# Attention and routed experts on one core: the last value rows read by a casting DMA, the routing steps moved within the first head pair, the gathered rows transposed one score group later

## The chip, the cores and the metric

The kernel runs on one core of one Trainium2 chip. The metric is the device time of one execution in microseconds (us). Each engine of the core works through its own list of instructions in order: TensorE (PE: matmuls and, beside them, weight loads), VectorE (DVE), ScalarE (ACT), GpSimd (POOL) and SyncE (SP, which here only issues DMAs). They wait for each other through semaphores. DMAs are issued from SP, ACT and POOL; those of POOL run on the queue that the profile calls software_dynamic, those of SP and ACT on hardware_dynamic queues.

## The reference

```python
scores = scale * np.matmul(q, k.transpose(0, 1, 3, 2))       # q, k, v: 8 x 8 x 576 x 64, float32
scores = scores + bias.transpose(2, 0, 1)[None, :, :, :]     # bias from |i - j| through a table of 32 buckets
attn = np.exp(scores - max) / (sum + 1e-09)
x = np.matmul(attn, v)                                       # laid out as 4608 tokens x 512
expert_idx = token_ids * np.int64(2654435761) % np.int64(E)  # E = 8 experts
for e in range(E):                                           # rows of expert e
    out[mask] = np.maximum(xe @ w1[e], 0.0) @ w2[e]          # w1: 512 x 1024, w2: 1024 x 512
```

Eight batches of eight heads go through attention; each of the 4608 resulting token rows then goes through the two matrices of one expert, which the token's id alone decides.

## The kernel before, in words

**Attention.** The work goes by head pairs: n = 0 to 31 is batch n // 4, pair m = n % 4 of its heads. For each pair, `scores` (line 484) makes score blocks in four groups g = 0 to 3, each in one of two PSUM buffers `ps`; ACT takes the exp of each group into `att` (lines 513 and 507). `band` (line 518) multiplies the blocks near the diagonal by the exp of the bias, from `ebd` (line 532), on DVE. `av_steps(n)` (line 560) multiplies `att` with the values in two halves (token tiles 0 to 2, then 3 and 4), divides by the row sums and writes `x_all` (lines 579, 589, 590); it is a generator, and the main loop (line 812) advances it by counted matmuls between the score groups of the next pair. So the order of all five engines is written out by hand (`tc.manual_schedule`), and each engine keeps it.

**Loads.** q, k and v come in as fp32, four pairs ahead, on SP (`load`, `load_v`); DVE casts q and k to fp16 (`cast_q`, `cast_k`, lines 274 and 283), PE transposes them (lines 457 and 472), DVE copies the results to `qt` and `kz` (lines 465, 478, 479). ACT casts the first 512 value rows of each head to `vt` (line 289). The last 64 value rows of all heads of a batch come in by `load_vs` (line 257) to an fp32 buffer `vsf` and are cast by POOL in `cast_vs` (line 264) to `vs`, which has one buffer for even and one for odd batches. For batch b + 1 the load stands in the loop at pair m = 1 of batch b and the cast at m = 3; the first matmul that reads it is that of `av_steps(4b + 4)`, advanced during pair 4b + 5.

**Routing.** `route` (line 296) is a generator too: it takes the expert of each token from the ids (`te`, line 299), casts and transposes them (`tef`, `tps`, `ef`), makes one-hot columns (`oh`, line 327), counts them with two matmuls (line 338), a scan (line 342) and a subtraction (line 348), and ends in `ds2`, the slot of each token. Before the main loop it is advanced to the subtraction; the rest comes one step a pair from n = 5. From pair 13 on POOL scatters the tokens' names into `t_id` by 40 indirect DMAs (`name_slot`, line 618), each behind a `pace` copy (line 603) that waits for a reciprocal `rcp` of the pair. At n = 28 SP loads the finished list as `xid` (line 836).

**The hand-over.** SP stores the attention rows of a batch to `t_x` (`store`, line 631), for batch 6 at pair 29. At n = 30 POOL gathers the first expert's 640 rows in five chunks of 128 (`gather`, line 151), from batches 0 to 6. In pair 31 `first_rows` (line 421) transposes chunks 1 to 4 on PE (`xr`) and copies them to `xt0` on DVE. After the loop, `first_slots` (line 432) adds the rows of the last batch straight from `x_all` by one-hot matmuls (`xin`). `aux` tiles (`pq`, `pk`, `px`, `tps`, `xr`, `xin`) share two PSUM buffers in turn.

**Experts.** For each expert, eight groups of matmuls `hps` (line 964), relu on ACT, five groups `ops` (line 988), copies on DVE and scattered stores on POOL (line 996).

Of the kernel before, what the change touches and what calls it, by code (L numbers as in the profile page):

```python
# [11 lines left out]
F32 = mybir.dt.float32  # L12
F16 = mybir.dt.float16
I32 = mybir.dt.int32
# [17 lines left out]
def kernel(  # L32
# [160 lines left out]
    with tc.tile_pool(name="at", bufs=1) as at, tc.tile_pool(  # L193
# [16 lines left out]
        kf = [at.tile([PB, 2, 2 * NBLK, D], F32, name=f"kf{i}")  # L210
              for i in range(4)]
        vf = [at.tile([P, 2, NDUO, D], F32, name=f"vf{i}") for i in range(4)]
        vsf = [at.tile([P, NPAIR, D], F32, name=f"vsf{i}") for i in range(2)]
        vt = [at.tile([P, 2 * (NDUO * VN + VO)], F16, name=f"vt{i}")
              for i in range(4)]
        vs = [at.tile([P, NPAIR, VW], F16, name=f"vs{i}") for i in range(2)]
# [37 lines left out]
                    ),  # L254
                )

        def load_vs(b, eng=nc.sync):
            for hh in range(2):
                eng.dma_start(
                    out=vsf[b % 2][D * hh : D * hh + D, :, :],  # L260
                    in_=v[b, hh::2, NB4:].transpose([1, 0, 2]),
                )

        def cast_vs(b):
            for hh in range(2):
                c0 = hh * HP
                nc.gpsimd.tensor_copy(  # L267
                    out=vs[b % 2][D * hh : D * hh + D, :, c0 : c0 + D],
                    in_=vsf[b % 2][D * hh : D * hh + D, :, :],
                )  # L270

        def cast_q(n):
# [21 lines left out]
            )  # L294

        def route():
            rev = raw[:, :, 0].rearrange("b (u o) -> b o u", o=2)[:, :, ::-1]
            for h0, w, u0 in ((0, UA, 0), (QW, UB, UA)):
                nc.vector.tensor_scalar(
                    out=te[:, h0 : h0 + 2 * w].rearrange(  # L300
                        "b (o u) -> b o u", o=2
                    ),
                    in0=rev[:, :, u0 : u0 + w],
                    scalar1=E - 1, scalar2=None, op0=ALU.bitwise_and,
                )
            yield
            nc.gpsimd.memset(tef[:, :].bitcast(I32), 0)
            nc.vector.tensor_copy(out=tef[:B, :], in_=te[:, :])
            yield
            tps = aux([P, NIT, P], F16, "tps")  # L310
            for t in range(NIT):
                nc.tensor.transpose(
                    out=tps[:, t, :], in_=tef[:, i_first[t] : i_first[t] + P],
                    identity=ident[:, :P],
                )
            nc.vector.tensor_tensor(
                out=ef[:, :].rearrange("p (b t) -> p t b", b=B),
                in0=tps[:, :, :B],
                in1=msk[:, :NGT].rearrange("p (b t) -> p t b", b=B),
                op=ALU.add,  # L320
            )
            keep = at.tile([P, E, NGT], F32, name="keep")
            nc.gpsimd.memset(keep[:, :, :], 1.0)
            nc.gpsimd.memset(keep[:, :, 0:1], 0.0)
            yield
            oh = at.tile([P, E, NGT], F16, name="oh")
            nc.vector.tensor_tensor(
                out=oh[:, :, :],
                in0=ef[:, :].unsqueeze(1).to_broadcast([P, E, NGT]),
                in1=msk[:, NGT : NGT + E].unsqueeze(2).to_broadcast([P, E, NGT]),  # L330
                op=ALU.is_equal,
            )
            yield
            EN = E * NGT
            ohf = oh[:, :, :].rearrange("p e g -> p (e g)")
            rps = atp.tile([P, 3, 512], F32, name="rps", tag="ps", bufs=2,
                           space=bass.MemoryType.PSUM)
            nc.tensor.matmul(out=rps[:, 0, :EN], lhsT=cnt[:, P:], rhs=ohf)
            nc.tensor.matmul(out=rps[:, 1, :EN], lhsT=cnt[:, :P], rhs=ohf)
            inc = at.tile([P, E, NGT], F32, name="inc")  # L340
            incf = inc[:, :, :].rearrange("p e g -> p (e g)")
            nc.vector.tensor_tensor_scan(
                out=incf, data0=keep[:, :, :].rearrange("p e g -> p (e g)"),
                data1=rps[:, 0, :EN], initial=0.0, op0=ALU.mult, op1=ALU.add,
            )
            rnk = at.tile([P, E, NGT], F32, name="rnk")
            rnkf = rnk[:, :, :].rearrange("p e g -> p (e g)")
            nc.vector.tensor_tensor(
                out=rnkf, in0=incf, in1=rps[:, 1, :EN], op=ALU.subtract
            )  # L350
            yield
            mx = at.tile([P, 1], F32, name="mx")
            nc.vector.tensor_reduce(
                out=mx[:, :], in_=inc[:, :, NGT - 1],
                axis=mybir.AxisListType.X, op=ALU.max,
            )
            yield
            mxl = at.tile([P, 1], F32, name="mxl")
            nc.vector.tensor_reduce(
                out=mxl[:, :], in_=inc[:, :, NIT - 1],  # L360
                axis=mybir.AxisListType.X, op=ALU.max,
            )
# [27 lines left out]
            yield  # L390
            nc.vector.scalar_tensor_tensor(
                out=ds2[:, :], in0=ovf[:, :], scalar=float(BIG),
                in1=sel[:, :], op0=ALU.mult, op1=ALU.add,
            )
            yield
# [272 lines left out]
        load(0, "qk")  # L668
        load(1, "q")

        def z_init(i, eng=nc.vector):
            eng.memset(kz[i][D:P, :S].bitcast(I32), 0)
            eng.memset(kz[i][:D, S:].bitcast(I32), 0)

        idle = at.tile([P, 512], F16, name="idle")
        nc.vector.memset(idle[:, :].bitcast(I32), 0)
# [36 lines left out]
                )  # L713

        z_init(1)
        FH = FW // 2
        for i in range(2):
            nc.tensor.matmul(
# [41 lines left out]
                )  # L760

        routing = route()
        advance(routing, 1)
        cast_q(0)
        advance(routing, 1)
        cast_k(0)
        load_bias(nc.scalar, 0, 1, 0)
        load_bias(nc.sync, 0, 1, 1)
        transpose_q(0)
        advance(routing, 2)  # L770
        v_init(0)
        vs_init(0)
        transpose_k(0)
        advance(routing, 1)
        load_vs(0, nc.gpsimd)
        z_init(2, nc.gpsimd)
        for i in range(1, 4):
            v_init(i)
        nobody = at.tile([P, NSLOT // P, 2], I32, name="nobody")
        nc.gpsimd.memset(nobody[:, :, :], BIG)  # L780
        load_v(0)
        cast_q(1)
        cast_k(1)
        nc.gpsimd.tensor_copy(out=pace[:, :], in_=kh[1][:1, 0, 0, 0:1])
        for b2 in range(2):
            load_bias(nc.gpsimd, 1, 2, b2)
        cast_vs(0)
        for b2 in range(2):
            load_bias(nc.gpsimd, 2, NPAIR, b2)
        load(1, "v")  # L790
# [21 lines left out]
        for n in range(NP + 1):  # L812
            av = iter(())
            if n > 0:
                av = av_steps(n - 1, finish if n == NP else None)
            if n == NP:
                first_slots(0, NPT - 1)
                advance(av, 99)
                first_slots(NPT - 1, NPT)
# [5 lines left out]
                vs_init(1)  # L825
            if n == 2:
                make_ebs()
            if b + 1 < B and m == 1:
                load_vs(b + 1)
            if b + 1 < B and m == 3:  # L830
                cast_vs(b + 1)
            if n >= 8 and pairs[n][1] == 0:
                store(pairs[n - 8][0], 0, NIT)
            if n == 28:
# [8 lines left out]
            for g in range(NSG + 1):  # L843
# [5 lines left out]
                if n == NP - 2 and g == 0:  # L849
                    gather(0, B - 1)  # L850
                if n == NP - 1:
                    for sc in ((), (1,), (2, 3), (4,))[g]:
                        first_rows(sc)
                if n == 16 and g == 0 or NP - 2 <= n and g in (0, 1, 3):
                    next(hotting, None)
                if n == 0:
                    if g == 1:
                        transpose_q(1)
                        transpose_k(1)
                        band(n, 0)  # L860
                    elif g == 2:
                        band(n, 1)
                        band(n, 2)
                    elif g == 3:
                        cast_v(0)
                        band(n, 3)
# [23 lines left out]
                elif g == 0:  # L890
                    if 2 < n < NP - 1:
                        transpose_k(n + 1)
                    low_bands(n - 1)
                    advance(av, 12)
                elif g == 1:
                    if n == 2:
                        cast_v(2)
                        load_v(6)
                        advance(av, 15)
                        transpose_k(3)  # L900
                        cast_q(4)
                    if n + 2 < NP:
# [1 line left out]
                    if 2 < n < NP - 1:  # L904
                        cast_v(n + 1)
                    if n > 2:
                        advance(av, 15)
                    band(n, 0)
                elif g == 2:
                    if n == 2:  # L910
# [232 lines left out]
```

## Time and profile before

| what | value |
|---|---|
| timed runs | 370.37, 370.32, 369.44 us; median 370.32 |
| the profiled execution | 370.93 us; its span 369.1 us |
| granted TensorE clock | 0.988 |
| PE busy | 323.6 us, 88% |
| DVE busy | 219.1 us, 59% |
| ACT busy | 236.8 us, 64% |
| POOL busy | 188.3 us, 51% |
| DMA | 66.01 MB, mean 179 GB/s |

The busy shares are means over stages with different limits: a head until the first exp (12.13 us), the attention (to 209.27 us, when the last exp ends), and the experts (from 214.08 us). The profile numbers lines as in the kernel printed above. A row of the timeline gives the start, the duration, the engine, the line, the operation, output and inputs, and in brackets the idle time that the engine had before it with what ended it. A wait for several semaphores is put down to the one that came last. "PEld" is the weight load, "issue" is time in which an engine waited for nothing that the profile shows.

### The profile page before, as it was taken

Reading aid. Unit: us, or ns where it says so; the run is one execution under the profiler, and the core shown is the slowest. Engines: PE = TensorE matmul, PEld = TensorE weight load, DVE = VectorE, ACT = ScalarE, POOL = GpSimd, SP = SyncE. Lnnn points to the kernel's source line nnn. Section 1 sums busy time; section 2 is a strip of 40 time slices with the busy share of each in tenths; the row PEclk is TensorE's granted clock in tenths of the full one; section 3 lists DMA queues with packets and bytes.
Section 4 is the critical chain, followed back from the end, with each engine's and each line's share of the span. In section 5 each row is a group of like instructions: output and inputs, shape, how many; then the busy total and the mean of one; then the engine's idle time right before and its main releaser. Section 6 shows DMA issues by size and latency. Waiting matters only on the chain.

```text
span 369.1 us, 8870 instructions
## 1 busy us (share of the span) xinstructions
PE 323.6 (88%) x3461; PEld 216.9 (59%) x3461; DVE 219.1 (59%) x590; ACT 236.8 (64%) x262; POOL 188.3 (51%) x304
## 2 busy tenths in 40 slices
PE   6777898888989888878877789999999999999991
PEld 2455675666666666656654665656565656565650
DVE  5978999999999999998977612121212121212121
ACT  2676898889999998978889334545454545454520
POOL 8631010131158848848822346688777777632232
PEclk9998999999999999999999999999999999999996
DMA  8999997898968898999935126589999999996112
GB/s 178 225 241 236 232 219 188 202 210 209 205 157 197 174 213 182 186 216 192 161 81 74 52 96 127 185 130 179 282 223 234 221 242 227 209 213 144 69 60 84
DMA packets 125477, 66.01 MB, mean 179 GB/s; under 512 B 86277, under 2 KB 117646, under 8 KB 125426
## 3 DMA queue, kind: packets, MB, share of 16 engines
q0 software_dynamic: 19680, 31.87, 42.2%
q1 hardware_dynamic: 105346, 33.25, 38.3%
q8 instruction: 29, 0.48, 0.5%
q10 hardware_dynamic: 400, 0.25, 0.3%
q14 instruction: 22, 0.18, 0.1%
HBM read 68.28 MB, written 15.30 MB: 226 GB/s over the span
## 4 chain that ended last, share of the span: by engine, by line
PE 49%; DVE 16%; DMA 14%; issue 7%; POOL 6%; ACT 5%; SPq 1%; POOLq 0%; ACTq 0%; DVEq 0%
PE ops L988 19%; PE hps L964 18%; DVE att L532 6%; PE px L579 4%; PE ps L502 4%; DMA vf<-in_v_dram 3%; DMA t_id<-pay,ds 3%; DVE x_all L590 3%; ACT att L513 3%; POOL t_id L619 2%; DMA t_x<-x_all 2%; PE xps L941 2%; ACT vt L289 2%; DMA ebd<-t_f 1%; DVE rcp L589 1%
## 5 line engine op out<-in xcount | busy, mean ns | idle before, releaser
L513 ACT ACTIVATE att<-ps 128x1536 f16<-128x1536 f32 x96 | 138.5, 1449 | 31.0 <-PE ps L502 17.7
L502 PE MATMUL ps<-qt,kz 128*128 128x512 f16 (+1 forms) x576 | 92.3, 288 | 22.4 <-ACT att L513 21.2
L995 DVE COPY ok<-ops 128x512 f32<-128x512 f32 x40 | 27.7, 692 | 120.3 <-PE ops L988 119.0
L579 PEld LDWEIGHTS <-att 128*128 128x128 f16 x1440 | 74.9, 98 | 25.3 <-issue 5.7
L579 PE MATMUL px<-vt,att 128*128 128x98 f16 x1280 | 81.4, 207 | 3.2 <-DVE kz L479 1.4
L988 PE MATMUL ops<-w2t,h 128*128 128x512 f16 x320 | 74.9, 379 | 0.0
L970 ACT ACTIVATE h<-hps 128x640 f16<-128x640 f32 x64 | 45.0, 704 | 41.9 <-PE hps L964 35.0
L532 DVE TENSOR_TENSOR att<-att,ebd 128x384 f16<-128x384 f16 (+2 forms) x192 | 70.3, 394 | 1.6 <-DMA ebd<-t_f 0.7
L964 PEld LDWEIGHTS <-w1t 128*128 128x128 f16 x512 | 50.1, 98 | 21.6 <-issue 1.1
L996 POOL DMA_INDIRECT out_dram<-ok,xid x40 | 39.5, 989 | 44.8 <-DVE ok L995 34.8
L964 PE MATMUL hps<-xpt,w1t 128*128 128x320 f16 x448 | 62.0, 299 | 0.0
L502 PEld LDWEIGHTS <-kz 128*128 128x128 f16 x576 | 36.2, 98 | 39.2 <-issue 25.8
L153 POOL DMA_INDIRECT xg<-t_x,xid x40 | 41.2, 1031 | 18.8 <-DMA t_x<-x_all 8.5
L988 PEld LDWEIGHTS <-h 128*128 128x128 f16 x320 | 30.1, 98 | 29.9
L619 POOL DMA_INDIRECT t_id<-pay,ds x40 | 41.6, 1041 | 8.8 <-issue 7.0
L945 ACT ACTIVATE xpt<-xps 128x512 f16<-128x512 f16 x35 | 20.1, 596 | 37.1 <-PE xps L941 37.1
L579 PE MATMUL px<-vs,att 128*128 128x132 f16 x160 | 35.6, 222 | 2.8 <-POOL vs L267 2.6
L590 DVE TENSOR_TENSOR x_all<-px,rcp 128x384 f16<-128x384 f32 x64 | 31.4, 491 | 2.2
L603 POOL COPY pace<-rcp 1x1 f32<-1x1 f32 x39 | 9.5, 244 | 42.3 <-DVE rcp L589 42.0
L267 POOL CAST vs<-vsf 64x256 f16<-64x256 f32 x16 | 8.1, 508 | 43.2 <-DMA vsf<-in_v_dram 25.3
L507 ACT ACTIVATE att<-ps 128x576 f16<-128x576 f32 x32 | 20.9, 653 | 2.7 <-PE ps L502 2.7
L289 ACT ACTIVATE vt<-vf 128x512 f16<-128x512 f32 x32 | 19.9, 623 | 0.0
(85 smaller groups left out, 266.4 us busy)
## 6 DMA issues: line engine op xcount, KB each, us to landing
qf<-in_q_dram SPq DMA_DIRECT2D x32, 288.0 KB
kf<-in_k_dram SPq DMA_DIRECT2D x32, 288.0 KB
vf<-in_v_dram SPq DMA_DIRECT2D x64, 128.0 KB
w1t<-in_moe_w_dram POOLq DMA_DIRECT2D x6, 1024.0 KB, 11.4
w2t<-in_moe_w_dram POOLq DMA_DIRECT2D x6, 1024.0 KB
t_x<-x_all SPq DMA_DIRECT2D x7, 512.0 KB
w1t<-in_moe_w_dram POOLq DMA_DIRECT2D x8, 256.0 KB
w2t<-in_moe_w_dram POOLq DMA_DIRECT2D x8, 256.0 KB, 9.5
```

What stands on the lines that cost most here:

```text
L153: nc.gpsimd.indirect_dma_start(out=xg[e % 3][:, sc, :], out_offset=None, in_=x_d.ap()[: S * nb, :], in_offset=bass.IndirectOffsetOnAxis(ap ...
L502: nc.tensor.matmul(out=out_ap, lhsT=z[:, k0 : k0 + P], rhs=rhs, start=True, stop=True,)
L513: nc.scalar.activation(out=att[:, 3 * g : 3 * g + 3, :QW], in_=ps[:, :, :], func=AF.Exp, bias=0.0, scale=scale,)
L532: nc.vector.tensor_tensor(out=a, in0=a, in1=ebd[:, :, m, :, a0 + w0 : a1 + w0].transpose([0, 2, 1, 3]), op=ALU.mult,)
L579: nc.tensor.matmul(out=px[:, ii, o : o + w], lhsT=lhsT, rhs=rhs, start=(y == 0), stop=(y == len(todo) - 1), skip_group_check=True,)
L590: nc.vector.tensor_tensor(out=x_all[:, b, its[0] : its[0] + ni, P * m : P * m + P].rearrange("p t (h d) -> p t h d", h=2), in0=pv[:, :, :, ...
L619: i = nc.gpsimd.indirect_dma_start(out=id_d.ap()[:, :], out_offset=bass.IndirectOffsetOnAxis(ap=ds2[:, g : g + 1], axis=0), in_=pay[:, g, ...
L964: nc.tensor.matmul(out=hps[:, nr, :NR], lhsT=w1h[:, kt, ts(ft, P)], rhs=xt[e][:, kt, ts(nr, NR)], start=(kt == 0), stop=(kt == NPT - 1),)
L970: nc.scalar.activation(out=h1[:, ft, :].rearrange("p (r n) -> p r n", r=NRC), in_=hps[:, :, :NR], func=AF.Relu, bias=0.0, scale=1.0,)
L988: nc.tensor.matmul(out=ops[:, :], lhsT=h1[:, ft, ts(kc, P)], rhs=w2h[:, ft, :], start=(ft == 0), stop=(ft == NFT - 1),)
L995: nc.vector.tensor_copy(out=ok[:, :], in_=ops[:, :])
L996: so = nc.gpsimd.indirect_dma_start(out=out[:, :], out_offset=bass.IndirectOffsetOnAxis(ap=xid[:, NSC * e + kc, 1:2], axis=0), in_=ok[:, : ...
```

## The change

Four things are edited.

1. The last value rows. `vsf` and `cast_vs` go. `load_vs` is issued from POOL and writes fp16 straight to `vs`; it stands at pair m = 2.
2. The start. `route` sets its constants on POOL at once, and its steps stand behind the q and k casts of pair 0: one step ahead of `transpose_k(0)`, one behind it, two behind the first scores and one behind the third. The two counting matmuls write `aux` tiles (`tot`, `low`) instead of a `ps` buffer. `kz[2]` is zeroed by DVE instead of POOL, and the bias of pair 1 is loaded on POOL before the `pace` copy that waits for `kh[1]`.
3. Pairs 2 and 3: `av_steps` is not advanced in group 0, but by 27 steps in group 1.
4. The end: `first_rows(1)` stands in group 2 of pair 31, chunks 2 and 3 in group 3, chunk 4 behind the loop.

```diff
-        vsf = [at.tile([P, NPAIR, D], F32, name=f"vsf{i}") for i in range(2)]
...
-        def load_vs(b, eng=nc.sync):
-            for hh in range(2):
-                eng.dma_start(
-                    out=vsf[b % 2][D * hh : D * hh + D, :, :],
-                    in_=v[b, hh::2, NB4:].transpose([1, 0, 2]),
-                )
-
-        def cast_vs(b):
+        def load_vs(b):
             for hh in range(2):
                 c0 = hh * HP
-                nc.gpsimd.tensor_copy(
+                nc.gpsimd.dma_start(
                     out=vs[b % 2][D * hh : D * hh + D, :, c0 : c0 + D],
-                    in_=vsf[b % 2][D * hh : D * hh + D, :, :],
+                    in_=v[b, hh::2, NB4:].transpose([1, 0, 2]),
                 )
...
-            rps = atp.tile([P, 3, 512], F32, name="rps", tag="ps", bufs=2,
-                           space=bass.MemoryType.PSUM)
-            nc.tensor.matmul(out=rps[:, 0, :EN], lhsT=cnt[:, P:], rhs=ohf)
-            nc.tensor.matmul(out=rps[:, 1, :EN], lhsT=cnt[:, :P], rhs=ohf)
+            tot = aux([P, EN], F32, "tot")
+            nc.tensor.matmul(out=tot[:, :], lhsT=cnt[:, P:], rhs=ohf)
+            low = aux([P, EN], F32, "low")
+            nc.tensor.matmul(out=low[:, :], lhsT=cnt[:, :P], rhs=ohf)
...
         z_init(1)
+        z_init(2)
...
         routing = route()
-        advance(routing, 1)
         cast_q(0)
-        advance(routing, 1)
         cast_k(0)
...
         transpose_q(0)
-        advance(routing, 2)
+        advance(routing, 1)
         v_init(0)
         vs_init(0)
         transpose_k(0)
         advance(routing, 1)
-        load_vs(0, nc.gpsimd)
-        z_init(2, nc.gpsimd)
-        for i in range(1, 4):
-            v_init(i)
+        load_vs(0)
+        v_init(1)
+        v_init(2)
+        for b2 in range(2):
+            load_bias(nc.gpsimd, 1, 2, b2)
+        v_init(3)
...
         nc.gpsimd.tensor_copy(out=pace[:, :], in_=kh[1][:1, 0, 0, 0:1])
-        for b2 in range(2):
-            load_bias(nc.gpsimd, 1, 2, b2)
-        cast_vs(0)
...
             if n == NP:
+                first_rows(NSLOT // P // E - 1)
                 first_slots(0, NPT - 1)
...
-            if b + 1 < B and m == 1:
+            if b + 1 < B and m == 2:
                 load_vs(b + 1)
-            if b + 1 < B and m == 3:
-                cast_vs(b + 1)
...
-                    for sc in ((), (1,), (2, 3), (4,))[g]:
+                    for sc in ((), (), (1,), (2, 3))[g]:
                         first_rows(sc)
...
                 if n == 0:
-                    if g == 1:
+                    if g == 0:
+                        advance(routing, 2)
+                    elif g == 1:
...
                         band(n, 2)
+                        advance(routing, 1)
...
                     low_bands(n - 1)
-                    advance(av, 12)
+                    if n > 3:
+                        advance(av, 12)
                 elif g == 1:
                     if n == 2:
...
-                        advance(av, 15)
+                        advance(av, 27)
...
-                        advance(av, 15)
+                        advance(av, 27 if n == 3 else 15)
```

More of the change, by code (lines that the diff above doesn't have):

```diff
@@ L296, in route @@
         def route():
+            nc.gpsimd.memset(tef[:, :].bitcast(I32), 0)
+            keep = at.tile([P, E, NGT], F32, name="keep")
+            nc.gpsimd.memset(keep[:, :, :], 1.0)
+            nc.gpsimd.memset(keep[:, :, 0:1], 0.0)
             rev = raw[:, :, 0].rearrange("b (u o) -> b o u", o=2)[:, :, ::-1]
@@ L306, in route @@
             yield
-            nc.gpsimd.memset(tef[:, :].bitcast(I32), 0)
             nc.vector.tensor_copy(out=tef[:B, :], in_=te[:, :])
@@ L321, in route @@
             )
-            keep = at.tile([P, E, NGT], F32, name="keep")
-            nc.gpsimd.memset(keep[:, :, :], 1.0)
-            nc.gpsimd.memset(keep[:, :, 0:1], 0.0)
             yield
@@ L343, in route @@
                 out=incf, data0=keep[:, :, :].rearrange("p e g -> p (e g)"),
-                data1=rps[:, 0, :EN], initial=0.0, op0=ALU.mult, op1=ALU.add,
+                data1=tot[:, :], initial=0.0, op0=ALU.mult, op1=ALU.add,
             )
@@ L348, in route @@
             nc.vector.tensor_tensor(
-                out=rnkf, in0=incf, in1=rps[:, 1, :EN], op=ALU.subtract
+                out=rnkf, in0=incf, in1=low[:, :], op=ALU.subtract
             )
@@ L669, with z_init @@
         load(1, "q")
-        def z_init(i, eng=nc.vector):
-            eng.memset(kz[i][D:P, :S].bitcast(I32), 0)
-            eng.memset(kz[i][:D, S:].bitcast(I32), 0)
+        def z_init(i):
+            nc.vector.memset(kz[i][D:P, :S].bitcast(I32), 0)
+            nc.vector.memset(kz[i][:D, S:].bitcast(I32), 0)
         idle = at.tile([P, 512], F16, name="idle")
```

## The prediction

> **What bounds the kernel now.** I read the page's busy shares first, then ScalarE's timeline through the attention, then the busy time by stage, then POOL's timeline and the chain of waits around the gaps. The span of 369.1 us has three stages: a head of 12.13 us before the first exp, 32 head pairs until the last exp ends at 209.27, and the expert stage. From the first hps matmul at 214.08 TensorE is busy 146.73 of 147.2 us, and the tail behind it is a copy and a scatter. Nothing in the change touches that, so a gain must come out of the first 214 us.
>
> By stage (stretch, length, then busy us of PE, PE loads, DVE, ACT, POOL with counts, then granted clock, DMA share, GB/s):
>
> ```profile
> 6.00:12.10 6.10, 4.73 (x25) 2.07 (x24) 5.81 (x12) 0.18 (x1) 3.92 (x10) 1.00 1.20 257
> ...
> 17.20:24.10 6.90, 5.00 (x76) 3.67 (x75) 5.38 (x16) 5.24 (x7) 4.21 (x9) 1.00 1.06 262
> 24.10:31.80 7.70, 6.03 (x88) 4.27 (x88) 7.05 (x21) 5.79 (x7) 1.45 (x3) 1.00 1.02 244
> 31.80:39.55 7.75, 6.74 (x81) 4.78 (x78) 6.47 (x19) 5.30 (x6) 0.00 (x0) 0.78 1.07 221
> ...
> 45.60:75.30 29.70, 25.81 (x385) 19.18 (x382) 28.91 (x88) 26.48 (x26) 3.95 (x13) 1.00 0.87 204
> ...
> 163.10:170.50 7.40, 5.27 (x81) 3.91 (x79) 5.53 (x16) 5.30 (x6) 5.00 (x8) 1.00 1.02 230
> ```
>
> An undisturbed pair takes 5.76 us (exp of pair 14 begins at 98.72, of pair 15 at 104.48), and there ACT and DVE are both almost full (DVE 28.91 of 29.70). Pairs 1, 2, 3 take 6.89, 7.74 and 7.73 us, pair 25 takes 7.40 and pair 29 takes 7.08. Those five and the last pair are the loss. Two of them come from POOL; its timeline, and those of PE and ACT behind it, show how (start, us, what; in brackets the idle time before it and what ended it):
>
> ```profile
> 183.32 0.97 POOL L619 DMA_INDIRECT t_id<-pay,ds  x1 [0.16 <-issue]
> 184.29 0.63 POOL L267 CAST vs<-vsf 64x256 f16<-64x256 f32 x1
> 189.55 0.42 POOL L267 CAST vs<-vsf 64x256 f16<-64x256 f32 x1 [4.62 <-DMA t_id<-pay,ds]
> 190.04 0.53 POOL L603 COPY pace<-rcp 1x1 f32<-1x1 f32 x1
> 190.72 0.99 POOL L619 DMA_INDIRECT t_id<-pay,ds  x1 [0.16 <-POOL pace L603]
> 200.18 1.15 POOL L153 DMA_INDIRECT xg<-t_x,xid  x1 [8.47 <-DMA t_x<-x_all]
> ```
> ```profile
> 190.03 0.22 PE L579 MATMUL px<-vs,att 128*128 128x132 f16 x1 [1.23 <-POOL vs L267]
> ...
> 191.06 1.45 ACT L513 ACTIVATE att<-ps 128x1536 f16<-128x1536 f32 x1 [1.37 <-PE ps L502]
> ...
> 204.41 0.40 PE L424 MATMUL xr<-ident,xg 128*128 128x128 f16 x4 [2.21 <-DMA xg<-t_x,xid]
> ...
> 206.17 1.45 ACT L513 ACTIVATE att<-ps 128x1536 f16<-128x1536 f32 x1 [2.37 <-PE ps L502]
> ```
>
> The second cast of a batch's last value rows waits for slot scatters (t_id) that have nothing to do with its data: 3.94, 4.45, 4.71, 4.62 us in four batches. In the built program that cast does carry waits on all scatters issued since the batch before. In pairs 25 and 29 the px matmul then waits 1.39 and 1.23 us for it, and the exp behind it 1.69 and 1.37. The same delay puts the last scatter at 190.72; SP's load of xid waits for it and is issued at 193.07, the store behind it at 193.54, so the gather starts at 200.18 and PE stands still for its second chunk.
>
> **What the Trainium skill says.** (1) "DMA: Bandwidth & Descriptors", section on SWDGE vs HWDGE vs iDMA: only DMAs issued from GpSimd can change the type, so these loads leave SP's queue for POOL's. The trace agrees as far as it goes: the casting weight loads are on the software queue. (2) "SBUF — State Buffer", section on the two separate sides: a VectorE operation in a two-port mode locks GpSimd out while it writes descriptors; 0.62 us becomes some 3.1. Here the 64 KB load from POOL took 0.64 us at 4.9 us, and the weight loads take 0.53 to 0.99 with DVE 95% busy: present, but small. (3) The first page, section on the anatomy of one DMA: about 2.0 us plus bytes over 436 GB/s, so 2.15 us for 64 KB (estimate). The trace has no landing for such a load from POOL; scatters land after 6.0 and weight loads after 9.5 to 11.4, so the page's price is a lower end. (4) "TensorE: Matmul & The Clock Gate", section on what is happening: after a quiet window of 3.4 us the clock halves. The trace agrees roughly: from 33 to 35 us the granted clock is 0.50, after a stretch with gaps.
>
> **The change, part by part.**
>
> *Value rows.* 16 POOL casts (8.1 us busy, 43.2 idle before them) and 14 loads on SP go; 14 more loads go to POOL (two existed), 0.64 to 1.0 us each, 9 to 14 us in all, or 1.3 to 2.0 per four pairs (23.0 us). POOL does its scatters, pace copies and weight issues in 5.2 us of 5.76 a pair (117.43 to 122.67), so they fit: four pairs need about 22.5. Behind a load on POOL wait the weight load, the pace copy and the scatters; none is needed within the pair. Each load also waits for the old reader of vs (two pairs back) and for the DMA eight places earlier, some 10 us old. It is issued three pairs (17.3 us) before its first use; landing taken as 6 us (2.15 to 11.4): hidden. SP loses work: nothing, SP is hidden behind four buffers. Gain: 1.69 + 1.37 less the 0.25 that such a group waits anyway (0 to 0.56 in the other pairs), twice: **2.6** (2.0 to 3.0).
>
> *Gather and last group.* With POOL in step, the last scatter needs only rcp of pair 26 (178.97), lands at about 186, and the store needs x_all of pair 27 (written by 186.82): it goes out near 187, not 193.54, and the gather starts 6.6 us sooner in the old clock, at about 193.6. Its five chunks (1.3 us apart, 2.8 to land) are in by 201.8, ahead of every first_rows in either order. So the shift by one group costs and gains nothing by itself then; if the gather stayed late, the shift alone would save the 2.21 at the second group but leave the fifth chunk, landing at about 208.4. What goes is PE's waits of 2.21, 0.76 and, for x_all that comes late through them, 0.34: 3.31; the transposes that hid in those gaps (0.4 each) partly come back: **2.6** (0.5 to 3.4).
>
> *Head.* Seven steps of routing take 4.00 us of DVE (0.92, 1.05, 0.23, 0.49, 0.82, 0.49). Of these 2.69 lie ahead of the kz copies at 10.08; after, only te's 0.92 does. kz2's memsets come to DVE (0.6), into its idle time before 6.08: nothing. qh can start at 5.5 if q has landed (it ran at 6.93 without a wait, so by then at the latest; k by 8.38). With early data kz starts at about 8.0 and the first exp comes 2.1 us sooner; with the latest, 0.2 later. But scan and subtraction (1.31) now stand between pair 0's bands on DVE, so its av starts only some 0.4 sooner. Matmul low waits for kz1 to free its buffer, under an exp of 1.45: nothing. The bias of pair 1 is issued at about 9.2, not behind kh1 at 13.63; its wait (0.66 on DVE, behind it px 1.42 and an exp 1.66) goes: +0.5. Its 192 KB take 0.75 us at 257 GB/s beside the first v load; vt at 16.68 has no wait, taken at 0.2 loss. In pairs 2 and 3 scores now precede av: the exps' waits of 0.67 and 2.03 go, but av's 27 matmuls (1.5 us) come back ahead of the third group: +1.3 of 2.7, less if the clock still drops. Sum 2.0, from which I take 0.4 off because DVE is nearly full here: its idle time from 6.0 to 39.55 is 0.29 + 0.28 + 1.52 + 0.65 + 1.28 = 4.0. Value **1.6** (-0.5 to 3.5).
>
> Sum 2.6 + 2.6 + 1.6 = 6.8: 369.1 becomes 362.3. The median of the timed runs is 370.32, 1.2 above this span; the forecast for the median is 363.5.
>
> **Rivals.** *The head gives nothing.* DVE is full and later steps take back what the first exp gains. For it: DVE's 5.81 of 6.10. Then 369.1 - 5.2 + 1.2 = 365.1. *The gather stays put.* POOL lags although the casts are gone (more software loads, each behind a busy DVE); then the fifth chunk at 208.4 anchors first_slots (208.8 against 209.15 now) whatever attention saves: 370.0, no change. Against it: the lag begins exactly at the four waits; before the first, at 101.31, POOL waits for DVE. *Slower: the rows land late.* If a load's lag and landing together exceed 17.3 us, PE waits for DMA where it waited for the cast. At 20 us it is 2.7 us in each of the four batches of POOL's busy stretch: 10.8, less 3.1 removed and 1.6 in the head, and no gain at the end: 376.4. Against it: the slowest landing seen is 11.6. *The edit does less than it says*: cannot be, the built program has no vsf and moves every step.
>
> **How the numbers follow.** Forecast with all three terms 0.61 (360.3 to 366); head nothing 0.18; a mix that leaves 2 to 3 us, the end giving little, 0.08; gather anchored 0.06; slower 0.07. The range 360.5 to 367.5 holds the first two and half of the mix; its low end is all upper bounds together (3.5 + 3.0 + 3.4 off 370.3). What a measurement of this kernel can tell from no change is about 0.3%, 1.1 us: faster 0.87, same 0.06, slower 0.07.
>
> **What would show it.** Right: no wait of px for vs and none of POOL for t_id at the value rows; exp starts of pairs 25 and 29 with their successors 5.8 to 6.2 us apart; the gather at least 5 us ahead of the first xr, and no wait before xr; the first exp at 10 to 11 us, pair 4 beginning near 38. Wrong: a px wait on a vs load, the gather still near 200, pairs 1 to 3 as long as now, or vt waiting for vf near 15 us.

## The result

The kernel after takes 364.6 us in the median (four runs, 363.8 to 366.15), the kernel before 370.35 (four runs, 369.44 to 371.51): a ratio of 0.985, interval 0.980 to 0.989. The two profiled executions have spans of 363.2 and 369.1 us, so 5.9 us are to be explained. The first hps matmul of the experts comes at 207.01 instead of 214.08; the front is 7.07 us shorter, and 1.1 of it is given back behind the last scatter. Ratios, here and below, leave out executions more than 1.5% above the fastest of their kernel; medians do not.

| stretch of the two profiles | before | after | gain | forecast |
|---|---|---|---|---|
| start of pair 5 (head) | 45.57 | 43.72 | 1.85 | 1.6 |
| pair 5 to pair 31 (value rows) | 155.44 | 152.53 | 2.90 | 2.6 |
| first exp of pair 31 to first hps (gather, last group) | 13.08 | 10.76 | 2.32 | 2.6 |
| first hps to the issue of the last scatter | 148.19 | 148.18 | 0.01 | 0 |
| issue of the last scatter to the end | 6.9 | 8.0 | -1.1 | 0 |

POOL's timeline of the kernel after, at the place shown for the kernel before:

```profile
167.41 1.34 POOL L259 DMA_DIRECT2D vs<-in_v_dram  x2
...
174.49 0.18 POOL L595 COPY pace<-rcp 1x1 f32<-1x1 f32 x1 [0.73 <-DVE rcp L581]
175.22 0.98 POOL L611 DMA_INDIRECT t_id<-pay,ds  x1 [0.55 <-issue]
191.95 1.06 POOL L153 DMA_INDIRECT xg<-t_x,xid  x1 [15.75 <-DMA t_x<-x_all]
...
197.41 1.01 POOL L153 DMA_INDIRECT xg<-t_x,xid  x1 [0.30 <-issue]
```

No cast and no wait for scatters are left: the last scatter is issued at 175.22 instead of 190.72, the gather 8.2 us sooner. PE and ACT behind it:

```profile
198.61 0.39 PE L416 MATMUL xr<-ident,xg 128*128 128x128 f16 x4
...
200.09 0.39 PE L416 MATMUL xr<-ident,xg 128*128 128x128 f16 x4
200.82 0.38 PE L416 MATMUL xr<-ident,xg 128*128 128x128 f16 x4 [0.34 <-DVE x_all L582]
201.92 0.38 PE L416 MATMUL xr<-ident,xg 128*128 128x128 f16 x4 [0.72 <-DVE xt L420]
```

The waits for xg (2.21 and 0.76) are gone; a wait for a copy of xt (0.72) is new. By stage (start and end, length, busy us of PE, PE loads, DVE, ACT, POOL with counts, clock, DMA share, GB/s): the head, pairs 1 to 4, then 5 to 9, 25 and 28:

```profile
6.00:11.20 5.20, 3.54 (x20) 1.53 (x19) 4.02 (x10) 0.19 (x1) 2.71 (x6) 1.00 1.35 233
16.84:23.88 7.04, 5.76 (x78) 3.89 (x77) 6.19 (x19) 5.31 (x6) 3.03 (x7) 1.00 1.21 272
23.88:31.07 7.19, 5.68 (x88) 4.10 (x86) 7.00 (x21) 5.70 (x7) 0.00 (x0) 1.00 1.04 231
31.07:36.82 5.75, 5.42 (x80) 3.66 (x77) 5.56 (x17) 5.30 (x6) 0.00 (x0) 1.00 0.92 189
36.82:43.72 6.90, 5.40 (x82) 3.91 (x79) 6.70 (x20) 5.30 (x5) 1.86 (x4) 1.00 1.21 289
43.72:73.42 29.70, 25.80 (x384) 19.17 (x382) 28.91 (x88) 26.46 (x25) 3.44 (x12) 1.00 0.87 198
160.03:165.78 5.75, 5.01 (x80) 3.80 (x78) 5.48 (x17) 5.30 (x5) 4.56 (x7) 1.00 0.98 209
177.55:184.82 7.27, 5.60 (x82) 4.14 (x83) 7.00 (x21) 5.30 (x6) 0.00 (x0) 1.00 0.83 215
```

Pair 25 takes 5.75 instead of 7.40, pair 3 5.75 instead of 7.73. The steady stretch is what it was, DVE at 28.91 of 29.70. Two pairs became clearly longer: pair 4 (6.90, it took 6.02) and pair 28 (7.27, it took 5.76); pair 0 takes 5.60 instead of 5.06, so that of the 0.9 us by which the first exp is sooner only 0.20 are left at pair 2. Pair 28's timeline on SP, DVE, PE and ACT names a wait that the kernel before did not have:

```profile
168.07 1.38 SPq L228 DMA_DIRECT2D qf<-in_q_dram  x1
169.54 0.47 SPq L237 DMA_DIRECT2D kf<-in_k_dram  x1
170.11 5.90 SPq L249 DMA_DIRECT2D vf<-in_v_dram  x2
176.10 0.56 SPq L228 DMA_DIRECT2D qf<-in_q_dram  x1
...
176.56 0.56 DVE L266 CAST qh<-qf 96x768 f16<-96x768 f32 x1 [1.34 <-DMA qf<-in_q_dram]
...
178.95 0.67 PE L571 MATMUL px<-vt,att 128*128 128x98 f16 x8 [0.76 <-DVE qt L457]
180.57 1.45 ACT L505 ACTIVATE att<-ps 128x1536 f16<-128x1536 f32 x1 [1.56 <-PE ps L494]
```

This q was issued at 168.07 and wanted at 175.22. The kernel before issued the same load at 169.80 and cast it at 179.94 without a wait. The front's need moved 4.7 us, the load only 1.7: SP stands behind pairs of value loads that occupy its queue for 3.69 to 5.90 us here.

### The profile page after: what moved, and what is told of

It is laid out like the page before. It is cut to its first block, busy times and chain, and to the rows that moved or that the text cites. A ratio compares the mean times of both kernels' runs of the same rounds, so it can differ in the third digit from the quotient of the medians.

```text
span 363.2 us, 8845 instructions
## 1 busy us (share of the span) xinstructions
PE 322.0 (89%) x3461; PEld 215.9 (59%) x3461; DVE 216.7 (60%) x592; ACT 236.6 (65%) x262; POOL 189.3 (52%) x300
## 4 chain that ended last, share of the span: by engine, by line
PE 58%; ACT 15%; issue 9%; DMA 8%; DVE 7%; SPq 0%; POOLq 0%; POOL 0%; DVEq 0%; ACTq 0%
PE ops L981 19%; PE hps L957 19%; ACT att L505 11%; PE ps L494 10%; PE px L571 6%; ACT vt L281 4%; DMA vf<-in_v_dram 4%; DVE att L524 2%; PE xps L934 2%; DMA qf<-in_q_dram 2%; DMA kf<-in_k_dram 2%; PE pk L464 1%; DVE x_all L582 1%; DVE qh L266 1%; DVE qt L457 1%
## 5 line engine op out<-in xcount | busy, mean ns | idle before, releaser
L571 PEld LDWEIGHTS <-att 128*128 128x128 f16 x1440 | 73.4, 97 | 21.8 <-DVE qt L457 1.3
L571 PE MATMUL px<-vt,att 128*128 128x98 f16 x1280 | 79.8, 206 | 2.7 <-DVE qt L457 1.7
L524 DVE TENSOR_TENSOR att<-att,ebd 128x384 f16<-128x384 f16 (+2 forms) x192 | 68.5, 385 | 0.9
L611 POOL DMA_INDIRECT t_id<-pay,ds x40 | 44.5, 1113 | 11.1 <-issue 10.8
L595 POOL COPY pace<-rcp 1x1 f32<-1x1 f32 x39 | 7.7, 197 | 45.3 <-DVE rcp L581 45.1
L259 POOL DMA_DIRECT2D vs<-in_v_dram x16 | 10.5, 661 | 22.4 <-PE ps L494 21.9
```

The costliest lines, as they stand in the source:

```text
L524: nc.vector.tensor_tensor(out=a, in0=a, in1=ebd[:, :, m, :, a0 + w0 : a1 + w0].transpose([0, 2, 1, 3]), op=ALU.mult,)
L571: nc.tensor.matmul(out=px[:, ii, o : o + w], lhsT=lhsT, rhs=rhs, start=(y == 0), stop=(y == len(todo) - 1), skip_group_check=True,)
L611: i = nc.gpsimd.indirect_dma_start(out=id_d.ap()[:, :], out_offset=bass.IndirectOffsetOnAxis(ap=ds2[:, g : g + 1], axis=0), in_=pay[:, g, ...
```

## The experiments

Twelve runs were made on three chips, four together each time; two of them are the kernel after once more. Every ratio is to the kernel before on the same chip, whose median was 372.75, 387.95 and 385.67 us there. The chips differ so much that times are compared inside one group only. Each profile shows one execution, and that one need not be a typical one: it took 365.55 us where the median is 368.03 for the value rows alone, 370.07 where it is 372.43 for the head alone.

### First group: the parts alone, on a chip where the kernel before takes 372.75

**Value rows alone.** The kernel before with

```diff
-                nc.gpsimd.tensor_copy(
+                nc.gpsimd.dma_start(
                     out=vs[b % 2][D * hh : D * hh + D, :, c0 : c0 + D],
-                    in_=vsf[b % 2][D * hh : D * hh + D, :, :],
+                    in_=v[b, hh::2, NB4:].transpose([1, 0, 2]),
...
-            if b + 1 < B and m == 1:
+            if b + 1 < B and m == 2:
                 load_vs(b + 1)
-            if b + 1 < B and m == 3:
-                cast_vs(b + 1)
```

> The kernel before with only the value rows changed (casting load on POOL at pair m = 2, no POOL cast); head, pairs 2 and 3 and the end as before. Theory: this part alone removes the waits in pairs 25 and 29 (2.6 us) and, because POOL no longer lags, lets the gather start about 6 us sooner, so that PE's waits for gathered rows (2.21 + 0.76) go without any shift: front 5.2 us shorter, about 365.1. First exp still at 12.1, gather start near 194 to 197 and ahead of the first xr. Rival (the shift of the transposes is what removes the wait for gathered rows): only the 2.6 to 3.0 of pairs 25 and 29, about 367.5, with a PE wait of more than 1 us for xg left in the last pair.

Measured: 368.03, ratio 0.987 (0.982 to 0.993), span 363.7. PE and POOL at the end:

```profile
191.92 1.12 POOL L153 DMA_INDIRECT xg<-t_x,xid  x1 [14.03 <-DMA t_x<-x_all]
...
198.66 0.39 PE L416 MATMUL xr<-ident,xg 128*128 128x128 f16 x4
...
200.21 0.87 PE L416 MATMUL xr<-ident,xg 128*128 128x128 f16 x8
...
202.27 0.39 PE L416 MATMUL xr<-ident,xg 128*128 128x128 f16 x4
...
207.93 2.33 PE L953 MATMUL hps<-xt,w1t 128*128 128x320 f16 x16 [0.38 <-DVE xt L440]
```

The theory holds by the trace: this part alone moves the gather to 191.92 and removes the waits for xg without the shift, and the first hps stands at 207.93, 0.92 us behind that of the kernel after. (The time alone would not tell it from the rival, whose 367.5 is a ratio of 0.992.) The last pair takes 10.29 us to the first hps, 0.47 less than with the shift. The two parts of that can be read in all profiles: from the end of the last exp to the first hps it takes 4.8 us where all four chunks stand in the groups and 5.9 to 6.1 where chunk 4 stands behind the loop; the exps of the pair themselves take 0.79 longer in this run (5.48 against 4.69). Pairs 27 and 28 take 6.57 and 6.84 here, behind waits of DVE for qf of 0.76 and 1.03: the new wait needs neither the new head nor the shift. That the faster front brings it is argued, not shown: the run with casts on DVE, whose front is not faster, has such waits too, and the value loads around pair 28's q hold SP's queue longer in the kernel after (5.16 and 5.90 us) than in the kernel before (2.87 and 2.93).

**The head alone.** The kernel after with value rows and `first_rows` as in the kernel before; against the kernel before, its start and pairs 2 and 3 are edited, as here:

```diff
-        advance(routing, 1)
         cast_q(0)
-        advance(routing, 1)
         cast_k(0)
...
-                    advance(av, 12)
+                    if n > 3:
+                        advance(av, 12)
```

> The kernel after with value rows and first_rows as in the kernel before, so only the start (routing order, kz2, bias, counting tiles) and pairs 2 and 3 are changed. Theory: pair 5 begins 1.85 us sooner as in the kernel after, and nothing takes it back: 370.3 - 1.85 = 368.5; waits of 1.4 to 1.7 in pairs 25 and 29 and the wait of about 2.2 before the second xr stay. Rival (what the head gains is taken back at the end, because the gather hangs on loads and stores whose pace the head does not set): 370.3, no change.

Measured: 372.43, ratio 0.998 (0.995 to 1.001). Both expectations miss part of it. Pair 5 begins at 43.46, so the head gives what it should, and most of the gain is lost again, but not at the gather. The timeline of POOL, PE and ACT in pair 25, and the sums of the stretch behind the wait, in the order of the tables by stage:

```profile
164.09 0.40 POOL L267 CAST vs<-vsf 64x256 f16<-64x256 f32 x1 [4.21 <-DMA t_id<-pay,ds]
...
164.54 0.27 PE L579 MATMUL px<-vs,att 128*128 128x132 f16 x1 [2.64 <-POOL vs L267]
...
166.38 1.45 ACT L513 ACTIVATE att<-ps 128x1536 f16<-128x1536 f32 x1 [3.92 <-PE ps L502]
```
```profile
164.50:167.50 3.00, 2.96 (x23) 2.13 (x23) 0.00 (x0) 1.12 (x1) 2.41 (x4) 0.50 1.03 256
```

Pair 25 begins 2.08 us sooner than in the kernel before, but its cast only 0.61 sooner, so the wait for vs is 2.64 instead of 1.39. Behind it the granted clock is 0.50 for 3 us, which the kernel before does not have there, and so the exp waits 3.92 instead of 1.69 and pair 25 takes 9.75 us instead of 7.40. Pair 29 then takes 5.75 instead of 7.08, without a wait for vs. So in this profile the terms do not simply add: with the false wait in place, an earlier front is taken back there, in part by the wait and in part by the clock.

**The cast without its wait.** The fp32 buffer and the casts stay; from batch 1 on DVE casts, and in the program built from it these casts wait for their load alone:

```diff
-                nc.gpsimd.tensor_copy(
+                (nc.gpsimd.tensor_copy if b == 0 else nc.vector.tensor_copy)(
                     out=vs[b % 2][D * hh : D * hh + D, :, c0 : c0 + D],
```

> The kernel before with the fp32 buffer kept, but its casts from batch 1 on issued on DVE instead of POOL, at the same place in the loop; in this program they wait for their own load alone and for no scatter. Theory (the false wait on scatters is the whole cost, not the cast or the buffer): pairs 25 and 29 lose no time to vs, POOL keeps in step and the gather starts near 194 to 197; what is paid is 14 DVE casts of some 0.25 us, up to 3.5 us where DVE is full: 365 to 368.6. Rival (the cast and its load are late by themselves, or the order of the loads costs): px still waits for vs in pairs 25 and 29, no gain, 370 or more.

Measured: 373.97, ratio 1.001 (0.998 to 1.004): no gain, so the time is the rival's. The profiled execution took 376.01 at a clock of 0.980, so it is read for its order of events more than for its lengths. POOL no longer waits for scatters, and no px waits for vs. The last scatter is issued in pair 27, as in the kernel after (pair 29 in the kernel before). The gather is issued at 199.28, 8.9 us ahead of the first exp of pair 31 (0.82 in the kernel before), and from that exp to the first hps it takes 10.30 us: the loss of the last group is gone although the casts are still there. Part of that lead comes from pair 27, which takes 11.79 us here, but POOL's being in step does not: in the order of events it was the wait, not the cast, that delayed the scatters and with them the gather. What the DVE casts take back is plain too: 14 of them at 293 ns, and pairs 12, 16, 20 and 24, each behind two of them, take 6.23 to 6.36 where the kernel before takes 5.75 to 5.81. Waits for qf (0.96 at pair 3, 4.42 in pair 27) came on top. Together they cost about what the wait on POOL did, so what the wait alone costs, with the cast kept, is not shown in time.

**No shift.** The kernel after with

```diff
-                    for sc in ((), (), (1,), (2, 3))[g]:
+                    for sc in ((), (1,), (2, 3), (4,))[g]:
```

and no `first_rows` behind the loop.

> The kernel after with first_rows placed as in the kernel before (chunk 1 in group 1 of pair 31, chunks 2 and 3 in group 2, chunk 4 in group 3). Theory (as forecast: the gather comes more than 5 us ahead, so the shift is worth nothing): 364.6 within 0.8, no PE wait for xg. Rival (the shift carries the gain of the last group): 2 us slower, about 366.8, with PE waiting for xg in group 1.

Measured: 368.44, ratio 0.989 (0.984 to 0.995); the kernel after itself did not run in this group, and its ratio of 0.985 lies inside, so the time decides nothing. The profile shows when the shift could count. Here pair 25 took 8.34 us behind a wait of 1.66 for qf (and at a granted clock of 0.50 from 162 to 165 us), the store of batch 6 took 2.99 us to issue from 187.49, and the gather began at 196.25, only 2.3 us ahead of pair 31's first exp:

```profile
200.75 0.38 PE L416 MATMUL xr<-ident,xg 128*128 128x128 f16 x4 [0.99 <-DMA xg<-t_x,xid]
```

One wait of 0.99: that much the shift could have bought here, and where the gather is early it costs the 0.47 seen above. Both are read from single profiles.

### Second group: the limit behind it, where the kernel before takes 387.95

> The kernel after once more, on the chip on which the variants beside it run, so that they are compared with it there. Theory: ratio to before 0.985 as measured first (front 5 to 7 us shorter). If the waits on q loads late in the attention differ from chip to chip, the pair that is long (28 in the first profile, 7.27 us) will be another one or there will be several.

Measured: 377.61, ratio 0.971 (0.966 to 0.977), twice the gain of the first comparison. Waits for qf stand in pairs 26 and 27 (1.12 and 0.77), and the long pairs are several: 16 takes 6.63, 24 7.19, 26 to 28 6.33 to 6.60. The last pair takes 13.36 us to the first hps instead of 10.76, with no wait for xg (14.71 in the next run): PE stands 2.06 us for x_all, behind a reciprocal for which DVE waits 3.23 us; why it waits so long is open.

**Value rows and shift, old head.**

> The kernel before with the value rows changed and first_rows one group later; start and pairs 2 and 3 as before. Theory A (terms add): slower than the kernel after by the head's 1.85 us. Theory B (what the head gains is given back in pairs 25 to 28, where q is not loaded in time): within 0.8 us of the kernel after, with the sum of what pairs 25 to 28 take over 4 x 5.75 smaller here than in the kernel after.

Measured: 378.94, ratio 0.974 (0.969 to 0.979), 1.3 us above the kernel after. The intervals overlap, so the time does not settle whether the head counts on top of the rows. The profiles tell more about its size: pair 5 begins at 44.43 here, at 43.62 in the kernel after. Pairs 25 to 28 do not take less here (7.93, 6.51, 6.34, 6.61 against 5.78, 6.33, 6.41, 6.60), which speaks against theory B.

**q two pairs earlier.** The kernel after, and the kernel before, with

```diff
-            if 0 < n < NP - 4:
+            if 0 < n < 10:
                 load(n + 4, "qk" if n < 3 else "qkv")
+            elif 0 < n < NP - 4:
+                for y in {10: (14, 15), 11: (16,), 12: (17, 18)}.get(n, (n + 6,)):
+                    if y < NP:
+                        load(y, "q")
+                load(n + 4, "k")
+                load_v(n + 4)
```

> The kernel after with SP's loads of q issued two pairs earlier from pair 10 on (pair n loads q of pair n + 6 instead of n + 4, its buffer being free then); k, v, weights as they were, the same bytes in all. Theory (the new wait is q's short lead, 1.6 pairs, behind value loads that hold SP's queue 3 to 6 us each): no DVE wait for qf, pairs 25 to 28 take under 6.1 us each, 1.3 to 3 us faster than the kernel after on this chip. Rival (the DMA engines as such are full there, so a load moved forward only makes another late): the wait shows up at kf or vf, no gain.

> The kernel before with the same earlier loads of q. Theory (before, the front is slow enough for q to land): no change, 370 within 1, waits for vs in pairs 25 and 29 as before. Rival (q's lead is short whatever the change): faster by 1 us or more.

Measured: 377.06, ratio 0.973 (0.968 to 0.978), and for the kernel before 388.38, ratio 1.005 (1.002 to 1.009). DVE does not wait for qf any more, and no wait for kf or vf appears in its place, so a load issued earlier is there in time. Yet nothing is gained: pairs 24, 25 and 27 still take 7.22, 6.42 and 7.17. The kernel before is even 0.5% longer with it, and its profile breaks the expectation: no px waits for vs, and pairs 18, 25 and 30 take 9.94 to 9.99 us, each with stretches at a granted clock of 0.50. The list of waits in the attention from 105 us on shows what else holds the engines there (line, what it waited for, us in total, times, longest), first of the kernel after on this chip:

```profile
PE ps L494 <- ACT att L505: 9.9, 12, 1.2
PE ps L494 <- issue: 3.4, 4, 1.2
...
PE px L571 <- issue: 0.6, 2, 0.3
```

In the first profile of the same kernel the same list has no "issue" for PE, ACT or DVE in that stretch:

```profile
PE ps L494 <- ACT att L505: 12.1, 16, 1.0
PE px L571 <- DVE qt L457: 0.8, 1, 0.8
```

All eight profiles of this group and the next have "issue" waits of PE's matmuls and of ACT from 105 us on, and none of the other six has. So on these chips engines also stand still for something that the profile does not show, and q's wait is only one of several. That is a failed fix: q's lead explained pair 28 in one profile, not the time.

### Third group: the head split, and two attempts at more, where the kernel before takes 385.67

> The kernel after, as the base for the variants beside it on this chip. Theory: 0.985 of before where before is near 370, less where before is slower; pair 5 begins near 43.7, a qf wait of about 1 us or more once or twice in pairs 24 to 28.

Measured: 373.71, ratio 0.970 (0.966 to 0.974). Pair 5 begins at 43.67. No wait for qf here; the long pairs late in the attention (24: 7.15, 30: 7.90) have other causes, "issue" among them (4.6 us of PE, 2.0 of ACT). The qf wait of the expectation is missing.

**The old order in pairs 2 and 3, new start.**

```diff
-                    if n > 3:
-                        advance(av, 12)
+                    advance(av, 12)
...
-                        advance(av, 27 if n == 3 else 15)
+                        advance(av, 15)
```

> The kernel after with av of pairs 1 and 2 advanced in group 0 again (as before in pairs 2 and 3); the new start is kept. Theory (of the head's gain, the start is worth 0.2 us at pair 2 and the order in pairs 2 and 3 some 0.6): pairs 2 to 4 together take 20.4 us instead of 19.8, pair 5 begins near 44.3; the median within 1 us above the kernel after. Rival (the start alone carries the gain, as the first exp is 0.9 to 1.4 sooner): pair 5 begins near 43.7 as well.

Measured: 374.76, ratio 0.973 (0.967 to 0.980). Pairs 2 to 4 take 7.74 + 6.93 + 5.72 = 20.39, as the theory said, and pair 5 begins at 44.14. This is the firmest figure of the head: in the seven profiles with the new order these three pairs take 19.82 to 19.88, in the other three with the old order and a clock of 1.00 20.37 to 20.57.

**Two versions meant to beat both.** The first takes q's lead and drops the shift; the second also has, for pair 4,

```diff
-                    if n > 3:
+                    if n > 4:
                         advance(av, 12)
```

> The kernel after with q loaded two pairs earlier and with first_rows placed as in the kernel before. Theory: with the gather in time, the shift costs 0.47 us in the last pair (10.76 from its first exp to the first hps, 10.29 in the run of the value rows alone), and q's waits of 1 to 2 us go: 1.5 to 2.5 us faster than the kernel after on this chip. Rival (other loads are late in q's place, or the gather is late): no faster, and a wait for xg, kf or vf of over 0.5 us.

> The kernel of the run best_a, and in pair 4 too av is not advanced in group 0 but by 27 steps in group 1. Theory: pair 4's second exp no longer waits 1.2 us for scores behind av, so pair 5 begins 0.9 us sooner than in best_a. Rival (DVE is full here and the wait moves on to pair 5): pair 6 begins no sooner than in best_a.

Measured: 375.18 (0.974, 0.969 to 0.978) and 375.11 (0.973, 0.967 to 0.979) against 373.71: neither is faster than the kernel after. That q's waits are gone shows nowhere in the time, and the last pair, where 0.47 were to come back, takes 11.95 and 12.11 us against 11.13 with the shift: both profiles have a granted clock of 0.50 from 201.5 to 204.5 us, at its start, and the kernel after does not. So the two are not a fair trial of the shift. In the second, pair 4 does shorten, from 6.90 to 5.71, and pair 5 grows from 5.69 to 6.78. ACT's timeline there:

```profile
42.96 1.45 ACT L505 ACTIVATE att<-ps 128x1536 f16<-128x1536 f32 x1 [0.40 <-ACT att L499]
45.48 1.45 ACT L505 ACTIVATE att<-ps 128x1536 f16<-128x1536 f32 x1 [1.07 <-PE ps L494]
...
49.74 1.45 ACT L505 ACTIVATE att<-ps 128x1536 f16<-128x1536 f32 x1 [0.40 <-ACT att L499]
```

The wait of 1.20 in pair 4 became one of 1.07 in pair 5, and pair 6 begins at 49.74 (49.54 in the first version): the rival was right. Pairs 4 and 5 together take 12.48 us instead of 12.59, so the work that was put off was made up one pair later.

## Why the prediction was right

The forecast of 363.5 stands against 364.6, and the main mechanism was the one named. The number alone would not show it: the rival in which the head gives nothing stood at 365.1, which is nearer. The sizes by the prediction's own steps:

- **Value rows, 2.6: right, measured 2.90.** Pairs 25 and 29 give 1.65 and 1.33; no px waits for vs, POOL waits for no scatter. The 16 loads take 0.66 us each on POOL; the one landing that the trace records comes after 3.73 us, six in the run without the shift after 3.84 to 5.97, well inside the 17.3 us that they had. The Trainium skill ("DMA: Bandwidth & Descriptors", section on the anatomy of one DMA) gave 2.15 as an estimate, which was a lower end as taken. Small gains in other pairs add 1.4, most of it in pairs 11, 17, 22 and 26, whose waits of 0.39 to 0.53 before an exp the prediction took as staying; why they went is not shown. The new wait in pair 28 takes 1.51 off. The prediction had neither, and that the two nearly cancel is luck.
- **"SP loses work: nothing, SP is hidden behind four buffers": wrong.** The buffers don't hide SP. The q of pair 28's wait was issued 10.14 us ahead of its cast in the kernel before, but only 7.15 us ahead of when it was wanted in the kernel after: where the front is 4.7 us earlier and SP's queue only 1.7, DVE waits 1.34.
- **Gather and last group, 2.6: right, measured 2.32.** The gather, forecast at about 193.6, started at 191.95, 6.66 us ahead of the first xr. The waits 2.21 and 0.76 went; the wait for x_all (0.34), which was to go as well, stayed, and xt's 0.72 is new; "no wait before xr" did not come true. That the shift "costs and gains nothing by itself" was off by the 0.47 that it cost in this pair of profiles, where the gather is early.
- **Head, 1.6: the sum fits by luck.** 1.85 was measured in the first pair of profiles, but the executions differ. Pair 5 begins at 44.43, 44.52 and 44.54 in three profiles with the old head and a clock of 1.00 from 32 to 36 us, at 45.57 in the one profile of the kernel before, with a clock of 0.57 there. (The run with casts on DVE has the old head too, at 47.30, with a wait for q and a clock of 0.50 from 35 to 38 us; it is left out.) The stretch in the kernel before and in the run of the value rows alone:

```profile
32.00:36.00 4.00, 3.40 (x29) 2.33 (x28) 3.10 (x10) 1.97 (x2) 0.00 (x0) 0.57 1.15 206
32.00:36.00 4.00, 3.24 (x43) 2.17 (x41) 3.85 (x12) 2.78 (x3) 0.00 (x0) 1.00 0.98 198
```

  Seven profiles with the new head give 43.46 to 44.02, in the mean 43.74. So some 0.8 us go with the edit and 1.1 with the half clock of one profile. Of the 0.8, the order in pairs 2 and 3 is worth 0.5 (20.4 against 19.84 for pairs 2 to 4); the 0.2 or so left for the start are less than the 0.56 by which the seven differ. The first exp came at 11.24, 0.9 sooner and not at "10 to 11": kh waited 1.12 for k. The order's "+1.3" was sized on the profile with the half clock, and pair 4 gave 0.9 of it back. Pair 4 began at 36.82, not "near 38". Half clock between 32 and 39 us stands in two of six profiles with the old order and in none of eight with the new one; that the new order avoids it is not shown by so few.
- **The tail, 0: wrong by 1.1.** "Nothing in the change touches that" is true of the instructions and not of the time.

Of the rivals, the one in which the head gives nothing was near: the head alone is 0.998 of the kernel before. The gather did move, and the rows did not land late.

What stays open: why the tail is longer; what the "issue" waits on two chips are; why the small losses in pairs 11, 17, 22 and 26 went; whether the new q wait comes from the front or from SP's longer value loads; and whether the head adds time saved on top of the rows, where 1.3 us were seen with overlapping intervals.

## What to carry to other kernels

A wait that an instruction carries for events unrelated to its data costs twice: where it stands, and in everything queued behind it on its engine; here a cast of 0.4 us, which waited for 4.6, held up the gather that stands three pairs later. Look at such waits first, because as long as they stand, other gains run into them: in one profile a front that came 2.1 us sooner made the same wait 1.25 us longer, and a spell of half clock behind it took about 1 us more. When a front gets faster, check the lead of every load against the new need, and do not count a gain in one pair of profiles as the edit's before a second profile shows it, as with the half clock here.

## What the runs showed that was not expected

**A longer end.** From the issue of the last scatter to the end of the span: 6.8 to 7.2 us in the four profiles with the fp32 buffer, 7.7 to 8.3 in all ten with the casting load, also where both ran on one chip. In the first pair of profiles the last scatter itself takes 0.97 us, and the DMA share is down to 0.00 five us after its issue. The runs don't show what fills the time.

**Spells of half clock.** In ten of the fourteen profiles the granted clock falls to 0.50 once or more in the attention, each time for 3.4 or 6.8 us; the kernel after has none in its three profiles, the value rows alone none either. All eight pairs that take over 8 us (8.34 to 11.79) lie in such a spell. They come behind stretches in which PE has many gaps, such as the 3.5 us ahead of 164.5 in the run of the head alone, where PE was busy for 0.88. But like stretches differ: PE was busy 1.58 of the 3.4 us to 32.7 in the kernel before, with a spell behind it, and 1.51 of the same 3.4 us in the run of the value rows alone, without one. What decides is not shown. What one spell costs can be read once: 1.1 us in pairs 3 and 4 of the kernel before (7.73 + 6.02 against 6.93 + 5.71). The times of one kernel go with its mean clock, though not strictly: of the 35 executions of the kernel before in the first group, the eight with a mean clock of 0.980 or less all take over 374 us, and three of the four with 0.990 or more under 370.4.

**Chips differ, and with them the worth of the change.** On the chips where the kernel before takes 387.95 and 385.67 us, the ratio is 0.971 and 0.970 instead of 0.985. From the first hps to the last scatter, where the kernels are the same, it takes 148.1 to 148.3 us in the profiles of the first comparison and the first group and 150.0 to 151.8 on these two chips. The larger worth is not explained by the waits for vs: the one profile with the old value rows there (q two pairs earlier) takes 170.97 us from pair 5 to pair 31, the kernel after 156.88, and its long pairs have "issue" waits and half clock and no wait for vs.

**POOL's DMA issues beside a full VectorE.** The Trainium skill ("SBUF — State Buffer", section on the two separate sides) says that GpSimd is locked out of writing descriptors beside some VectorE operations, such as a copy, and that a DMA from GpSimd of some 0.62 us then takes some 3.1. Here issuing the 16 loads took 0.62 to 0.86 us of POOL each, 0.66 in the mean, with DVE 97% busy in the steady stretch: no issue shows such a lock, and the "present, but small" of the prediction is not shown either. How many of VectorE's operations there could take the lock the runs do not tell, and the landings (3.73 to 5.97 us) are too few to judge by.
